# A fused long-convolution and gated-GLU kernel: fewer inverse-stage matmuls by combining complex products on VectorE, other places for the up copies, and a new instruction order

## The chip, the cores and the metric

The kernel runs on one core of a Trainium2 chip. The metric is the device time of one execution in microseconds (us). A core has five engines with a queue each: TensorE (PE in the profile, its weight loads PEld), VectorE (DVE), ScalarE (ACT), GpSimd (POOL) and SyncE (SP). Each works through its own queue in order and waits at semaphores for the others. A chip can give TensorE less than its full clock. Runs in which it did so markedly, or that took over 1.5% longer than the fastest run of their kernel, are "slow", and are not compared with "fast" ones.

## The reference, cut to what matters

```python
xn = layernorm(q)                                  # 2048 x 640
# A: causal long convolution over the 2048 tokens, per channel, by FFT
kv = shift_conv(k, shift_k) * v
y  = irfft(rfft(pad(kv)) * rfft(pad(ssm_k)))[:2048] + kv * ssm_D
# B: gated GLU, inner width 1728
h  = sigmoid(xn @ w_gate) * (xn @ w_up)
out = q + xn * y + h @ w_down
```

## The kernel before: what the change touches

**Part A** is a two-step DFT done with matmuls, for ten groups of 64 channels (an index `idx` from 0 to 9). Stage 1 (products of 32 rows) and stage 2 (of 64 rows) go forward. Then VectorE multiplies the spectra of `kv` and of the filter. The inverse stage (128 rows) and the last stage (32 x 32 tiles) go back. **Part B** is done for four blocks of 512 tokens, with 14 chunks of the inner width each: five matmuls for gate, five for up, a sigmoid on ScalarE, a multiply on VectorE, and after all chunks the down projection. The two parts are interleaved on TensorE by hand: part A's short runs stand between the projections of part B.

The product of two complex numbers needs `re*re - im*im` and `re*im + im*re`. The real parts lie in partitions 0 to 63 and the imaginary ones in 64 to 127. Without `ZC`, VectorE makes only the four real products, and the inverse stage adds them up in its accumulation, with two matmuls per output. With `ZC`, VectorE also does the subtraction and the addition, in halves of 64 partitions, and one matmul is enough:

```python
def rec_prod(idx, pri):
    ...                                        # Q = re*im and im*re into buffer P
    for b in range(2):
        dve(n, 2, lambda b=b: nc.vector.tensor_tensor(X(b), X(b), H(b), ALU.mult), ...)
    if idx in PRM["ZC"]:
        for b in range(2):
            dve(n, 2, lambda b=b: nc.vector.tensor_tensor(X(b)[0:64], X(b)[0:64], X(b)[64:P], ALU.subtract), ...)
            dve(n, 2, lambda b=b: nc.vector.tensor_tensor(X(b)[64:P], Q(b)[0:64], Q(b)[64:P], ALU.add), ...)

def rec_st3(idx, pri):                         # the inverse stage
    ...
            for j in range(JS):
                nc.tensor.matmul(o, lhsT=tl[S_][:, b, 0, j, :], rhs=Ab[:, 2 if zc else 0, :], start=True, stop=zc)
                if not zc:
                    nc.tensor.matmul(o, lhsT=tl[Z][:, b, j, :], rhs=Ab[:, 1, :], start=False, stop=True)
```

There is one buffer `P` for products. Without `ZC` it is held until the inverse stage has read it; with `ZC` only until VectorE has combined it.

An up projection is either multiplied straight from its PSUM bank, or first copied into the GLU buffer `hT` and multiplied there. The copy lets the bank go without waiting for VectorE:

```python
elif fc in PRM["UP"] and PRM["UP0"] <= pri < PRM["UP1"]:
    act(512, ...sigmoid -> sig...)
    ev(512, lambda: hT[:, fc, :], lambda: pv(1), ...)                              # the copy
    dve(512, 2, ...tensor_tensor(hT[:, fc, :], sig, hT[:, fc, :], ALU.mult)...)
else:
    act(512, ...sigmoid -> sig...)
    dve(512, 1, ...tensor_tensor(hT[:, fc, :], sig, pv(1), ALU.mult)...)           # straight from PSUM
```

Gate and up share two projection banks (`g`); part A has three double banks (`c`).

The order is not found by the kernel at run time. Two lists of numbers, `ORDER` and `ON_DVE`, say in which order about 950 operations are recorded, and which evictions VectorE takes in place of ScalarE. A buffer or bank is handed to the next user in the recorded order.

## Time and profile before

| | before |
|---|---|
| time, median of 3 runs | 268.5 us (267.57 to 269.28) |
| profiled run | span 268.0 us, clock 0.997, fast |
| TensorE, VectorE, ScalarE busy | 252.1, 181.6, 166.4 us |
| projections of blocks 0, 1, 2, 3 | 30.7, 46.6, 46.3, 46.3 us |
| down projections of blocks 0, 1, 2 | 15.8, 23.9, 21.4 us |

The trace has only 4336 of the 4375 matmuls (39 records of projections are missing), so its busy time of TensorE is somewhat low. A stage here goes from the start of a block's first projection matmul on TensorE's timeline to the start of its first down matmul, or from that to the next block.

The prediction below shows the lines of busy shares, slices and groups. Two more views are used later. First, TensorE's waits: what waited, for which engine, buffer and line; then us in total, the number of waits, and the longest.

```profile
PE g L766 <- DVE hT L733: 1.7, 2, 1.4
PE g L766 <- issue: 1.3, 8, 0.2
PE g L766 <- ACT sig L731: 1.0, 2, 0.7
```

The eight "issue" waits of 0.16 us are no waits: each stands before a run that is one record short of a multiple of five, so a missing record of the trace leaves the hole. Second, the busy time by engine in the projections of blocks 1 and 3: window, length, busy us of TensorE, its weight loads, VectorE, ScalarE and GpSimd with their counts, then clock, DMA share and GB/s.

```profile
61.64:108.26 46.62, 44.49 (x830) 25.48 (x839) 45.59 (x86) 38.74 (x51) 0.00 (x0) 1.00 0.65 162
199.83:246.17 46.34, 45.39 (x965) 27.39 (x975) 23.90 (x35) 30.62 (x41) 0.00 (x0) 1.00 0.30 76
```

In block 1 VectorE is busy for 45.6 of 46.6 us, as full as TensorE. In block 3 it has half its time free.

### The profile page before, as it was taken

How to read it: one execution, taken by the hardware profiler on the slowest of the kernel's cores; microseconds unless marked ns; L12 is line 12 of the kernel's file. 1: busy time of each engine (PE TensorE's matmuls, PEld its weight loads, DVE VectorE, ACT ScalarE, POOL GpSimd, SP SyncE). 2: the span in 40 equal slices, each digit the busy share in tenths (PEclk: the TensorE clock that was granted, in tenths of full speed). 3: DMA queues.
4: the chain of work that ended last, by engine and by line, in shares of the span. 5: the costliest groups of instructions: out<-in, count | busy, mean ns of one | idle time of the engine just before them, and what ended most of it. 6: DMA issues, size and time to landing. Idle time of an engine off the chain costs nothing.

```text
span 268.0 us, 9684 instructions
## 1 busy us (share of the span) xinstructions
PE 252.1 (94%) x4336; PEld 156.3 (58%) x4375; DVE 181.6 (68%) x319; ACT 166.4 (62%) x245; POOL 0.7 (0%) x6
## 2 busy tenths in 40 slices
PE   8899967998999999899999999999999999999993
PEld 3754434774445665677755555577676655555672
DVE  5333375269999999987799988695725853535831
ACT  3644945996499989674357649554477785644200
POOL 1000000000000000000000000000000000000000
PEclk9999999999999999999999999999999999999998
DMA  6999999999937516999954146677723075301741
GB/s 179 326 292 215 230 201 214 156 152 209 227 114 249 96 33 192 181 153 147 140 170 136 62 83 194 166 213 101 192 87 81 5 198 156 76 2 41 185 129 48
DMA packets 90449, 40.41 MB, mean 151 GB/s; under 512 B 66592, under 2 KB 88040, under 8 KB 90088
## 3 DMA queue, kind: packets, MB, share of 16 engines
q1 hardware_dynamic: 90216, 39.47, 69.0%
q8 instruction: 34, 0.56, 0.9%
q10 hardware_dynamic: 192, 0.33, 0.4%
q14 instruction: 7, 0.06, 0.1%
HBM read 30.61 MB, written 5.24 MB: 134 GB/s over the span
## 4 chain that ended last, share of the span: by engine, by line
PE 57%; SPq 14%; DVE 13%; DMA 10%; issue 3%; ACT 0%; DVEq 0%
PE g L766 23%; PE g L782 15%; PE c L523 6%; SPq L445 6%; DMA acc<-in_A_q_dram 4%; PE c L607 4%; DMA w<-in_B_w_gate_dram 3%; DVE ta L473 3%; PE c L503 2%; PE c L575 2%; SPq L412 2%; DVE P L553 2%; PE c L577 2%; PE g L812 2%; DMA ht<-in_A_ssm_k_dram 2%
## 5 line engine op out<-in xcount | busy, mean ns | idle before, releaser
L766 PE MATMUL g<-xnT,w 128*128 128x512 bf16 x348 | 86.3, 379 | 4.8 <-DVE hT L733 1.4
L782 PE MATMUL g<-wd,hT 128*128 128x320 bf16 x448 | 64.9, 299 | 0.0
L766 PEld LDWEIGHTS <-w 128*128 128x128 bf16 x380 | 34.5, 98 | 40.1 <-issue 3.7
L782 PEld LDWEIGHTS <-hT 128*128 128x128 bf16 x448 | 42.3, 98 | 16.5
L316 ACT CAST S<-c 128x1024 bf16<-128x1024 f32 x33 | 32.7, 1020 | 16.1 <-PE c L523 16.1
L733 DVE TENSOR_TENSOR hT<-sig,g 128x512 bf16<-128x512 bf16 x32 | 21.9, 685 | 17.7 <-PE g L766 11.9
L766 PE MATMUL g<-xnT,V 128*128 128x512 bf16 x133 | 31.2, 379 | 1.3 <-DVE acc L794 0.4
L794 DVE TENSOR_TENSOR acc<-g,acc 128x320 bf16<-128x320 f32 x32 | 15.6, 489 | 24.5 <-PE g L782 24.4
L731 ACT ACTIVATE sig<-g 128x512 bf16<-128x512 f32 x32 | 19.2, 600 | 18.8 <-PE g L766 14.9
L523 PEld LDWEIGHTS <-Mt 64*128 64x128 f16 x1280 | 20.2, 95 | 10.6 <-issue 10.2
L523 PE MATMUL c<-T,Mt 64*128 64x64 bf16 x1280 | 23.4, 190 | 0.8 <-DVE S L317 0.8
L316 ACT CAST V<-c 128x1024 bf16<-128x1024 f32 x19 | 18.6, 1014 | 7.9 <-PE c L577 7.8
L766 PEld LDWEIGHTS <-V 128*128 128x128 bf16 x140 | 13.3, 97 | 16.5 <-issue 1.5
L575 PE MATMUL c<-At,S 128*128 128x128 f16 x160 | 19.6, 219 | 0.5 <-DVE S L556 0.3
L316 ACT CAST T<-c 128x1024 bf16<-128x1024 f32 x18 | 17.6, 1023 | 3.2 <-PE c L503 3.2
L577 PE MATMUL c<-At,P 128*128 128x128 f16 x160 | 19.6, 219 | 0.0
L725 ACT ACTIVATE sig<-g 128x512 bf16<-128x512 f32 x18 | 10.8, 602 | 10.9 <-PE g L766 9.8
L575 PEld LDWEIGHTS <-S 128*128 128x128 bf16 x160 | 15.5, 98 | 2.5 <-DVE S L556 1.5
L319 ACT ACTIVATE T<-c 128x1024 bf16<-128x1024 f32 x14 | 13.9, 1024 | 3.9 <-PE c L503 3.9
L577 PEld LDWEIGHTS <-P 128*128 128x128 bf16 x160 | 15.7, 98 | 0.9
L728 DVE TENSOR_TENSOR hT<-sig,hT 128x512 bf16<-128x512 bf16 x18 | 7.5, 424 | 12.6 <-ACT hT L316 12.5
L553 DVE TENSOR_TENSOR P<-S 64x1024 bf16<-64x1024 bf16 x20 | 13.7, 686 | 1.2 <-PE c L577 0.7
(85 smaller groups left out, 264.8 us busy)
## 6 DMA issues: line engine op xcount, KB each, us to landing
w<-in_B_w_gate_dram SPq DMA_DIRECT2D x7, 640.0 KB, 6.6
w<-in_B_w_up_dram SPq DMA_DIRECT2D x7, 640.0 KB, 4.8
kt<-in_A_k_dram SPq DMA_DIRECT2D x8, 320.0 KB, 6.0
vt<-in_A_v_dram SPq DMA_DIRECT2D x8, 320.0 KB, 6.7
xnd<-xq SPq DMA_DIRECT2D x4, 640.0 KB, 3.9
P<-S SPq DMA_DIRECT2D x10, 256.0 KB, 3.7
ht<-in_A_ssm_k_dram SPq DMA_DIRECT2D x16, 96.0 KB, 5.2
wd<-in_B_w_down_dram SPq DMA_DIRECT2D x3, 480.0 KB, 9.6
```

The lines of the kernel that those rows point to most:

```text
L316: fa = lambda: nc.scalar.copy(out=out_fn(), in_=in_fn())
L319: fa = lambda: nc.scalar.activation(out_fn(), in_fn(), ACT.Copy, scale=scale)
L445: dma(lambda e, g=g, p=p, c0=c0: e.dma_start(tl[b][g * N1:(g + 1) * N1, :, p, :], h3[:, c0 + j0:c0 + j1, :]), 32 * (j1 - j0), 128, w=[(b, ...
L523: nc.tensor.matmul(tl[c][:, b, 64 * kk:64 * kk + 64], lhsT=Mb[rows, k, 64 - 64 * r:192 - 64 * r], rhs=tl[T][rows, 2 * k + r].rearrange("p ...
L553: dve(n, 2, lambda a=a, o=o, b=b: nc.vector.tensor_tensor(Q(b)[a], X(b)[a], H(b)[o], ALU.mult), r=sr + ([(Z, b, 1)] if h else []), w=[(Z, ...
L575: nc.tensor.matmul(o, lhsT=tl[S_][:, b, 0, j, :], rhs=Ab[:, 2 if zc else 0, :], start=True, stop=zc)
L577: nc.tensor.matmul(o, lhsT=tl[Z][:, b, j, :], rhs=Ab[:, 1, :], start=False, stop=True)
L731: act(512, lambda: nc.scalar.activation(tl[sg][:], pv(0), ACT.Sigmoid), r=[pk(0)], w=[(sg,)], alloc=[(sg, "sig")], pri=pri - 2000)
L733: dve(512, 1, lambda: nc.vector.tensor_tensor(hT[:, fc, :], tl[sg][:], pv(1), ALU.mult), r=[pk(1), (sg,)], w=[(hk, fc)], pri=pri - 2000)
L766: nc.tensor.matmul(tl[c][:], lhsT=w()[:, k, o:o + P], rhs=tl[X][:, k, :], start=(k == 0), stop=(k == NC - 1))
L782: nc.tensor.matmul(tl[pd[i]][:, 0:320], lhsT=hT[:, fc, t4 * P:(t4 + 1) * P], rhs=wd[:, fc, 320 * i:320 * i + 320], start=(fc == 0), stop=( ...
L794: dve(320, 1, lambda i=i, m=m, pd=pd: nc.vector.tensor_tensor(acc[:, m, 320 * i:320 * i + 320], tl[pd[i]][:, 0:320], acc[:, m, 320 * i:320 ...
```

## The change

It has two intents. The first is to take 96 matmuls off TensorE and give 24 operations to VectorE, where that has room. The second is to put the up copies where they help. Both go with a wholly new recorded order.

```diff
-               SWAP=(5, 6, 7, 8, 9), UP=(1, 3, 5, 7, 9, 11), UP0=60.0, UP1=230.0, ZC=())
+               SWAP=(5, 6, 7, 8, 9), UP=(0, 1, 2, 3, 4, 5, 6, 7, 8, 9, 10, 11, 12), UP0=130.0, UP1=230.0,
+               ZC=(4, 5, 6, 7, 8, 9))
...
-            pe(490, 32, f, ...
+            pe(460, 32, f, ...          # estimates of durations: they set priorities; ORDER fixes the order
...
-    MG, MD = 215.2, 136.5    # the priorities that follow from these are what UP0 and UP1 are compared with
+    MG, MD = 213.5, 135.0
...
 ORDER = [
-    6, 0, 5, 1, 4, 2, 8, 7, 42, 11, 10, 13, 12, 9, 3, 14, 16, 71, 72, 15, 73, 74, 75, 91, 17, 86, 76, 96, 77, 104,
...
+    3, 6, 0, 5, 42, 1, 4, 2, 8, 7, 11, 10, 13, 12, 9, 14, 16, 71, 72, 15, 73, 74, 75, 91, 17, 86, 76, 96, 77, 104,
...                                      # the whole list differs; ON_DVE goes from 30 to 26 entries
```

Before, the odd chunks of blocks 1, 2 and 3 were copied (18 copies). After, chunks 7 to 12 of block 2 and all 13 full chunks of block 3 are (19 copies), and none in block 1.

## The prediction

> **What bounds the kernel now.** I read the page's busy shares and slices first, then the costliest groups, then the timeline of TensorE, then the waits.
>
> ```profile
> PE 252.1 (94%) x4336; PEld 156.3 (58%) x4375; DVE 181.6 (68%) x319; ACT 166.4 (62%) x245; POOL 0.7 (0%) x6
> ...
> PE   8899967998999999899999999999999999999993
> ...
> DVE  5333375269999999987799988695725853535831
> ACT  3644945996499989674357649554477785644200
> ...
> L733 DVE TENSOR_TENSOR hT<-sig,g 128x512 bf16<-128x512 bf16 x32 | 21.9, 685 | 17.7 <-PE g L766 11.9
> ...
> L316 ACT CAST V<-c 128x1024 bf16<-128x1024 f32 x19 | 18.6, 1014 | 7.9 <-PE c L577 7.8
> ...
> L577 PE MATMUL c<-At,P 128*128 128x128 f16 x160 | 19.6, 219 | 0.0
> ...
> L728 DVE TENSOR_TENSOR hT<-sig,hT 128x512 bf16<-128x512 bf16 x18 | 7.5, 424 | 12.6 <-ACT hT L316 12.5
> L553 DVE TENSOR_TENSOR P<-S 64x1024 bf16<-64x1024 bf16 x20 | 13.7, 686 | 1.2 <-PE c L577 0.7
> ```
>
> TensorE is busy in nearly every slice. Slices 10 to 17 (60 to 115 us) have VectorE full as well: there the two bind together. After slice 24 (160 us) VectorE is at 30 to 80% and TensorE alone sets the pace. So a TensorE instruction removed late is worth its whole issue time, and VectorE work added there is nearly free.
>
> "Busy" hides how fast matmuls issue, so I took start-to-start times from the timeline of TensorE.
>
> ```profile
> 115.63 0.22 PE L577 MATMUL c<-At,P 128*128 128x128 f16 x1
> 115.69 0.22 PE L575 MATMUL c<-At,S 128*128 128x128 f16 x1
> ...
> 149.75 3.40 PE L766 MATMUL g<-xnT,w 128*128 128x512 bf16 x15
> 153.08 0.64 PE L523 MATMUL c<-T,Mt 64*128 64x64 bf16 x32
> 153.65 0.69 PE L607 MATMUL c<-V,Bt 32*32 32x80 bf16 x64
> ...
> 201.00 1.57 PE L523 MATMUL c<-T,Mt 64*128 64x64 bf16 x96
> 202.51 1.25 PE L766 MATMUL g<-xnT,w 128*128 128x512 bf16 x4
> 203.60 1.11 PE L782 MATMUL g<-wd,hT 128*128 128x320 bf16 x7
> ```
>
> The 128-column matmuls of the inverse stage start 0.056 us apart (32 of them fill 115.57 to 117.36). The 219 ns of the group table is latency, not cost. The stage-2 runs show a fixed cost: 32 take 0.57 us, 96 take 1.51, so 0.0147 each and 0.10 per run. A projection run of 15 ahead of such a run takes 3.33 us where 15 at 213 ns are 3.20 (213 ns is the pace of the first block: 60 matmuls between 15.15 and 27.89 us). The projection run ahead of a down projection (five matmuls, one record missing) takes 1.09 and has no such surplus. I read it as about 0.11 us for going over to a run of 32- or 64-row products, and about as much once per stage-2 run.
>
> Real waits of TensorE are few. The largest pair is at the end of block 0:
>
> ```profile
> 37.14 1.02 PE L766 MATMUL g<-xnT,w 128*128 128x512 bf16 x4 [0.69 <-ACT sig L731]
> 39.59 3.40 PE L766 MATMUL g<-xnT,w 128*128 128x512 bf16 x15 [1.42 <-DVE hT L733]
> ```
>
> VectorE's timeline says why: the multiply of chunk 10 stands behind the 13 small instructions of the reciprocal root (35.96 to 38.5 us), which stand behind a table copy that waited for its load until 34.98. Other waits sum to about 6 us, the end after the last matmul to about 4.
>
> **What the Trainium skill says.** "TensorE: Matmul & The Clock Gate", section "Back-to-back issue gap", gives N/2.4 + 2.5 ns warm: 55.8 for 128 columns, where the trace has 56; for 512 it gives 216, the trace 213, and I use the trace. "Perfetto Trace Analysis", "Identifying the Most-Contended Engine", says matmul busy share is a poor measure because pipelined instructions overlap; the trace agrees (219 against 56). "VectorE: DVE Perf Modes", "Walkthrough: the 8-slice pipeline in each mode", has a two-tensor operation at two 16-bit elements per cycle at best, and at one with a PSUM operand. The trace agrees: 512 columns cost 424 ns from SBUF (L728) and 685 from PSUM (L733), and 64 partitions (L553) cost the same 686 ns as 128 (L556), so the half-height operations that the change adds are not cheap. "ScalarE: Activation LUTs", "What ACT_TABLE_LOAD costs", gives 186 + 0.833 N ns: 612 for 512 columns; the trace's up copies take 594.
>
> **The change part by part.** It is the diff's parameters, plus a wholly new instruction order. I counted instructions of both built programs per engine and multiplied by the durations above.
>
> 1. Complex product combined on VectorE for groups 4 to 9. Each inverse-stage unit goes from 16 to 8 matmuls, two units per group, six groups: 96 matmuls and 96 weight loads fewer; x 0.056 = **-5.4 us of TensorE**. VectorE gets 24 operations of 64x1024: x 0.686 = +16.5 us. Each group's chain from stage 2 to the inverse stage grows by 4 x 0.69 = 2.75 us, which hurts only if TensorE gets there first. The order puts the inverse stage of groups 5 to 9 well after the last stage-2 run of its group (12 to 38 us of TensorE work between), group 4 about 11.5 us.
>
> 2. Up copies. Before, six odd chunks of each of blocks 1, 2, 3 (18). After, none of block 1, six of the later chunks of block 2, all 13 of block 3 (19). One more copy on ScalarE, 0.6 us; one multiply of 0.424 for one of 0.685 on VectorE. The total hardly moves; the place does.
>
> 3. Evictions. VectorE gives up 4 stage-2, 5 stage-1 and some small ones and takes others, and takes three normalisations from ScalarE. With parts 1 and 2, VectorE's sum is 181.6 -> about 190.7, ScalarE's 166.4 -> about 171. Neither is near 260. In block 1's projections VectorE loses four evictions of 1.22, six multiplies of 0.424 and some others: about 8 us less where it was full. That stretch (61.6 to 108.3 us) holds about 45 us of TensorE work in 46.6: worth **-1.0 us**.
>
> 4. Order. Runs of TensorE work go from 158 to 134. Entries into 32- or 64-row runs fall from 53 to 39, stage-2 runs from 26 to 20: 20 x 0.11 = **-2.2 us**. The reciprocal root of block 0 no longer has the table copy ahead of it and its statistics end before chunk 10's sigmoid, so the wait of 2.1 us should shrink to 0.8: **-1.3**. Against it: two memsets (0.33 + 0.27) now precede the one that the warm-up matmuls need, and TensorE's start sets the first transposes: **+0.6**.
>
> 5. New waits. Input rows (about 1 MB) now load ahead of weights for chunks 4 to 7. With about 4 MB moved by 15 us in the trace before, these weights should land near 17 us, needed at 19.5; tight. Longer VectorE chains will also miss some slots. I allow **+1.3**.
>
> Sum: -5.4 - 1.0 - 2.2 - 1.3 + 0.6 + 1.3 = -8.0, so 268.5 -> 260.5 us.
>
> **Rivals.** First: VectorE becomes the bound. For it: it is at 95 to 99% from 60 to 110 and around 140 us, and gets 9 us more. Against: the additions fall from 115 us on, mostly where it idles, and block 1 is relieved. If group 4 and 5 run late, 264 to 267. Second: ScalarE. It takes 7 big evictions net and statistics in one lump during the first down projection; late sigmoids hold the two projection banks. Against: 62% busy, and its sum grows by under 5 us. If so, 263 to 265. Third: loads in the first 30 us come late, since the queues are full there; up to 3 us, about 263. Fourth: the order works better than I allow and no new wait appears: 258.
>
> **Range and chances.** The 5.4 us are an instruction count and alone are 2.0%, just at the limit; the run count adds 2.2 with a less sure unit. For less than 2% (above 263.1 us) new waits must eat about 3.9 us where I allow 1.3. I give 257.5 to 264.0; faster 0.77, same 0.20, slower 0.03.
>
> **What would show it.** Matmuls of the inverse stage 224 instead of 320, still 56 ns apart; TensorE busy near 245 us with its last slices unchanged; projections of block 1 about 2 us shorter; the wait near 37 us under 1 us; the first transpose at 6.9 instead of 6.28 us; no wait of TensorE on the combining operations above 1 us in total. It is wrong if TensorE waits several us on them or on projection banks, if single matmuls start further than 56 ns apart (weight loads of 98 ns binding), or if weights come late near 19 us.

## The result, and the profile after

The changed kernel took 259.97 us in the median of four runs, against 268.89 us for the kernel before in the same rounds. The result is correct. One of the four runs, the profiled one, was slow: 357.06 us at a mean granted clock of 0.661. The three fast ones took 257.36, 258.83 and 261.11 us. The ratio of the fast runs is 0.964, with an interval of 0.954 to 0.974: faster. All ratios here are those of the record, from fast runs of the same rounds, so not quite the ratio of the medians that are quoted. The prediction was 260.5 us, 257.5 to 264.0; the median of the three fast runs is 258.83.

As the first profile was slow, the changed kernel was run again, and all profile lines of "after" are from that run.

> The changed kernel again, because its first profile fell in the slow state. Theory (TensorE sets the pace, 96 matmuls and about 20 run entries fewer): 257.4 to 261.1 us as in the fast runs so far, ratio about 0.964; TensorE busy about 245 us; inverse-stage matmuls still 0.056 us apart; first transpose 0.6 us later than before (6.9); the wait near 37 us under 1 us; block 1's projections 2 us shorter than 46.6. Rival (the gain is removed waits, not removed matmuls): TensorE busy stays near 250 and its idle time falls by over 5 us.

Measured: 258.61 us (257.82 to 260.29), ratio 0.959 (0.951 to 0.967), profile fast with a span of 258.5 us. Line numbers of the changed kernel are two higher in its body (L766 is now L768, L577 is L579, and so on).

The page: busy shares, the slices, and groups.

```profile
PE 245.9 (95%) x4279; PEld 151.6 (59%) x4279; DVE 191.9 (74%) x339; ACT 169.9 (66%) x250; POOL 0.7 (0%) x6
...
PE   7889997999999999999999998999999999999993
...
DVE  5424364557899999988998789779978696959631
...
L735 DVE TENSOR_TENSOR hT<-sig,g 128x512 bf16<-128x512 bf16 x31 | 21.2, 686 | 17.3 <-PE g L768 17.3
...
L577 PE MATMUL c<-At,S 128*128 128x128 f16 x160 | 15.0, 219 | 0.4 <-issue 0.3
...
L579 PE MATMUL c<-At,P 128*128 128x128 f16 x64 | 7.8, 219 | 0.0
```

The inverse stage is 160 matmuls of the first kind, with 64 of the second kind left: 224 for 320. They still start about 0.055 us apart (eight of them fill 203.60 to 204.04). VectorE is now at 70% or more in 18 of the 24 slices after the sixteenth, where it had been in 13, and after the start TensorE's row of nines is broken only by one seven and one eight. The waits of TensorE:

```profile
PE g L814 <- DVE sig L803: 1.8, 1, 1.8
PE c L525 <- issue: 1.7, 1, 1.7
PE c L748 <- ACT sig L733: 0.8, 1, 0.8
PE g L768 <- ACT sig L733: 0.4, 1, 0.4
```

No wait on the combining operations (L562 and L564) is among them. The wait on the multiply hT is down from 1.7 to 0.2 us. New are a wait for the first sigmoid (L748) and one named "issue" in the middle of a stage-2 run. All listed waits together are 8.0 us; before they were 8.3 without the holes of missing records. So the 9.5 us between the two spans are hardly less waiting, they are less work on TensorE, and the rival named above for a1_after does not hold. The windows of blocks 1 and 3:

```profile
60.46:104.73 44.27, 44.04 (x842) 25.40 (x839) 41.67 (x79) 38.31 (x47) 0.00 (x0) 1.00 0.81 177
197.97:237.25 39.28, 39.26 (x762) 21.81 (x759) 30.88 (x49) 26.34 (x39) 0.00 (x0) 1.00 0.37 98
```

In both, TensorE's busy time is within 0.3 us of the length. Block 1's projections became 2.35 us shorter. Block 3's fell by 7.1 us, of which 3.1 reappear in the down projection of block 2, which took over some of its part-A work. The start is later, on the other hand: block 0's projections begin at 16.30 instead of 15.15 us. From the timeline of TensorE (start, length, work, and in brackets the idle time before it and its releaser):

```profile
6.89 0.74 PE L702 MATMUL c<-ident,xq 128*128 128x128 bf16 x5
...
15.47 1.00 PE L748 MATMUL c<-xnT,V 128*128 128x128 bf16 x15 [0.77 <-ACT sig L733]
...
153.64 0.93 PE L525 MATMUL c<-T,Mt 64*128 64x64 bf16 x51
156.26 0.83 PE L525 MATMUL c<-T,Mt 64*128 64x64 bf16 x45 [1.69 <-issue]
```

The first transpose starts at 6.89, as predicted. The second line was not predicted: the last matmuls of the first chunks are recorded behind the first sigmoid, which stands on ScalarE behind a table load (1.28 us in this trace). The last two lines are one run of 96 matmuls, cut in two by a wait that no semaphore explains; more on it below.

### The profile page after: what moved, and what is told of

Its sections match the earlier page's. It is cut to its first block, busy times and chain, and to the rows that moved or that the text cites. A ratio compares the mean times of both kernels' runs of the same rounds, so it can differ in the third digit from the quotient of the medians.

```text
span 355.3 us, 9555 instructions
## 1 busy us (share of the span) xinstructions
PE 346.1 (97%) x4279; PEld 185.5 (52%) x4279; DVE 193.9 (55%) x339; ACT 171.9 (48%) x250; POOL 0.7 (0%) x6
## 4 chain that ended last, share of the span: by engine, by line
PE 97%; ACT 1%; DVE 0%; issue 0%
PE g L768 48%; PE g L784 26%; PE c L525 8%; PE c L577 4%; PE c L505 3%; PE c L609 3%; PE g L814 2%; PE c L748 2%; PE c L579 1%; ACT xnT L317 1%; PE c L702 0%; ACT sig L733 0%; PE g L702 0%; ACT sig L722 0%; DVE acc L796 0%
## 5 line engine op out<-in xcount | busy, mean ns | idle before, releaser
L768 PE MATMUL g<-xnT,w 128*128 128x512 bf16 x380 | 128.8, 510 | 0.3 <-ACT sig L733 0.3
L784 PE MATMUL g<-wd,hT 128*128 128x320 bf16 x448 | 94.4, 387 | 0.0
L768 PEld LDWEIGHTS <-w 128*128 128x128 bf16 x380 | 43.9, 120 | 66.4 <-issue 64.5
L784 PEld LDWEIGHTS <-hT 128*128 128x128 bf16 x448 | 51.5, 118 | 35.0 <-issue 0.4
L735 DVE TENSOR_TENSOR hT<-sig,g 128x512 bf16<-128x512 bf16 x31 | 21.3, 687 | 47.6 <-PE g L768 47.3
L768 PE MATMUL g<-xnT,V 128*128 128x512 bf16 x140 | 46.7, 510 | 0.0
L525 PEld LDWEIGHTS <-Mt 64*128 64x128 f16 x1280 | 25.6, 104 | 10.0 <-issue 9.3
L768 PEld LDWEIGHTS <-V 128*128 128x128 bf16 x140 | 16.1, 119 | 25.7 <-issue 24.5
L525 PE MATMUL c<-T,Mt 64*128 64x64 bf16 x1280 | 28.4, 210 | 0.0
L320 ACT ACTIVATE T<-c 128x1024 bf16<-128x1024 f32 x18 | 17.8, 1025 | 6.8 <-PE c L505 6.8
L317 ACT CAST hT<-g 128x512 bf16<-128x512 f32 x19 | 11.1, 586 | 19.8 <-PE g L768 19.8
L577 PE MATMUL c<-At,S 128*128 128x128 f16 x160 | 20.7, 265 | 0.0
L577 PEld LDWEIGHTS <-S 128*128 128x128 bf16 x160 | 15.9, 118 | 3.8 <-issue 2.8
L470 DVE TENSOR_TENSOR tb<-kt,sT 128x1024 bf16<-128x1024 bf16 x20 | 13.7, 687 | 1.6 <-ACT kt L317 1.4
```

The costliest lines, as they stand in the source:

```text
L317: fa = lambda: nc.scalar.copy(out=out_fn(), in_=in_fn())
L320: fa = lambda: nc.scalar.activation(out_fn(), in_fn(), ACT.Copy, scale=scale)
L470: dve(1024, 2, lambda: nc.vector.tensor_tensor(tl[c][:], sl(tl[kb], 3 - m), sh(m), ALU.mult) if c != o else nc.vector.tensor_tensor(tl[c]. ...
L525: nc.tensor.matmul(tl[c][:, b, 64 * kk:64 * kk + 64], lhsT=Mb[rows, k, 64 - 64 * r:192 - 64 * r], rhs=tl[T][rows, 2 * k + r].rearrange("p ...
L735: dve(512, 1, lambda: nc.vector.tensor_tensor(hT[:, fc, :], tl[sg][:], pv(1), ALU.mult), r=[pk(1), (sg,)], w=[(hk, fc)], pri=pri - 2000)
L768: nc.tensor.matmul(tl[c][:], lhsT=w()[:, k, o:o + P], rhs=tl[X][:, k, :], start=(k == 0), stop=(k == NC - 1))
```

## The experiments

Theory: TensorE sets the pace from end to end, so the gain is the 96 matmuls, plus fewer visits to runs of 32- or 64-row products, plus a few waits; copies and order only have to keep new waits away. The rival is that one part alone, the order or the placing of the copies, makes the gain, or that the combining has a price on the path. A third view came up on the way: that the parts cannot be valued one by one.

All results, with the lengths of the projections of blocks 1, 2 and 3 from each profile:

| run | what it is | median us | ratio to before | 1 | 2 | 3 |
|---|---|---|---|---|---|---|
| before | | 268.5 | | 46.6 | 46.3 | 46.3 |
| a1_after | the changed kernel | 258.61 | 0.959 | 44.3 | 46.3 | 39.3 |
| a2_pe16 | after, 96 matmuls given back | 266.13 | 0.987 | 44.3 | 47.4 | 42.0 |
| b1_zc | before + combining, old order | 284.62 | 1.057 | 46.6 | 48.8 | 53.0 |
| b2_zclate | the same, inverse stages later | 299.64 | 1.117 | 46.6 | 53.5 | 63.4 |
| b3_up | before + new copies, old order | 273.46 | 1.016 | 50.0 | 48.9 | 46.4 |
| a3_order | new order, neither | 290.91 | 1.072 | 48.9 | 62.2 | 52.8 |
| a9_nozc | new order + new copies, no combining | 273.47 | 1.017 | 44.3 | 56.0 | 43.0 |
| a4_upold | new order + combining, old copies | 274.12 | 1.023 | 49.2 | 49.2 | 45.6 |
| a5b_noup | after without any copy | 273.58 | 1.017 | 44.3 | 49.5 | 49.0 |
| a7_up1 | after + copies of block 1 | 266.10 | 0.986 | 49.7 | 45.7 | 39.3 |
| a8_split | after, 8 more visits to 32-row runs | 262.32 | 0.976 | 44.3 | 46.3 | 39.5 |
| a6_start | after, earlier start | 258.49 | 0.964 | 44.3 | 48.5 | 39.3 |

Two of the four runs of a3_order, the profiled one among them, were slow, so its stages are only a hint; its ratio is from the fast runs (288.16 and 289.16 us). All other profiles in the table are fast; that of a1_after is of the slowest of its four runs (260.29 us). Where a part was brought into an order that was made without it, some operations had to be recorded earlier, since otherwise a buffer or bank never comes free. Such kernels are not the part alone; they are the part in a repaired order.

### The 96 matmuls given back (a2_pe16)

```diff
+                    if zc:
+                        nc.tensor.matmul(o, lhsT=tl[S_][:, b, 0, j, :], rhs=Ab[:, 2, :], start=True, stop=True)
                     nc.tensor.matmul(o, lhsT=tl[S_][:, b, 0, j, :], rhs=Ab[:, 2 if zc else 0, :], start=True, stop=zc)
```

Each matmul of the six groups is done twice, with the same result; combining, order and copies stay.

> The changed kernel with the 96 matmuls given back as doubles (each product of groups 4 to 9 issued twice into the same place, the second overwrites, so the result is right); VectorE's combining stays. Theory (TensorE bound): 96 x 0.056 = 5.4 us slower than the changed kernel, so about 264. Rival (these stages wait for VectorE anyway, or the gain is in the order): under 2.5 us slower.

Measured: 266.13 us, 7.5 more than the changed kernel in the same rounds; by the two profiles 265.1 - 258.5 = 6.6. Stage by stage from the traces: 16 more inverse matmuls in block 2's projections lengthened them by 1.1 us, 32 in its down projection by 2.3, 48 in block 3's projections by 2.67 (48 x 0.056 = 2.69). Block 3 has no listed wait in either trace, so that stage prices the matmul alone. The sum of the 0.056s is 5.4. The rest of the 6.6 (1.2) is mostly waits: a new one for an up copy in block 2 and one near the end,

```profile
168.33 3.40 PE L770 MATMUL g<-xnT,w 128*128 128x512 bf16 x15 [0.96 <-ACT hT L317]
...
251.82 8.45 PE L786 MATMUL g<-wd,hT 128*128 128x320 bf16 x61 [1.12 <-issue]
```

and a longer "issue" wait in the down projection of block 2 (0.79 instead of 0.32 us); against them stand shorter "issue" waits in block 2 (1.6 instead of 2.1) and a start 0.5 us earlier. So the theory's term holds at its unit, and the matmuls carry 5.4 of the 9.8 us between the two medians (268.44 and 258.61 in those rounds) directly.

### Combining in the old order (b1_zc, b2_zclate)

```diff
-  ... UP=(1, 3, 5, 7, 9, 11), UP0=60.0, UP1=230.0, ZC=())
+  ... UP=(1, 3, 5, 7, 9, 11), UP0=60.0, UP1=230.0, ZC=(4, 5, 6, 7, 8, 9))
 # ORDER: the four combining operations of a group right behind its products
```

> The kernel before with only the combining on VectorE for groups 4 to 9, each group's four operations put right behind its products in the old order. Theory: 5.4 us of TensorE less, but the old order has the inverse stage close behind the products of group 4 and VectorE full until 150 us, so 1 to 3 us come back as waits: 264 to 267. Rival one (VectorE not in the way at all): 263. Rival two (VectorE's 16.5 us bind): 268 or more.

Measured: 284.62 us, 16 us slower than before, though it has the same 96 matmuls fewer. My expectation failed badly; even the rival's "268 or more" was mild. The waits of TensorE, first line:

```profile
PE c L577 <- DVE S L564: 10.7, 6, 2.9
```

The inverse stages stand where products alone would have been ready. Each group's chain is 4 x 0.69 us longer, and TensorE stops for it, up to 2.9 us at a time. All listed waits of TensorE are 23.3 us, against 9.6 before. The clock adds to it: the trace has it at 0.50 in two stretches of 3.4 us, worth at most 3.4 of the 16 us. The wait on the combining is what the prediction had feared for groups 4 and 5, and the new order does not have it. So I made the inverse stages of groups 4 to 9 later by three items of TensorE's queue:

> As b1_zc (the old order, combining on VectorE for groups 4 to 9), but the inverse stages of these groups stand three TensorE work items later. Theory (what cost b1_zc 14 us is the longer chain from product to inverse stage, met by an inverse stage that stood right behind it): waits of TensorE on the combining fall from 24 us to under 8 and the time to 268 to 274. Rival (VectorE's added 16.5 us bind by their amount): still 280 or more.

Measured: 299.64 us. (The 24 us in the expectation are nearly all listed waits of TensorE in b1_zc; those on the combining were the 10.7 above.) The aimed-at waits fell to about 1 us, and the kernel became slower still. The waits of ScalarE tell why (same columns as above, with ScalarE waiting):

```profile
ACT V L318 <- PE c L577: 37.3, 10, 9.0
```

ScalarE's evictions of the inverse stage kept their old places in its queue, to within one. They now waited 37.3 us for the later matmuls, the sigmoids behind them waited too, and TensorE stopped for projection banks. I conclude that an operation cannot be moved on one engine alone: each queue is in order, and the whole neighbourhood has to move. A run with the neighbourhood moved as well was not made. The theory fell, and with it any hope of pricing the combining by itself in the old order. The clock of this profile was 0.96: it was at 0.50 in five stretches, 24 us in all, so up to 12 of the 31 us are clock.

### New copies in the old order (b3_up), and the order without the combining (a3_order, a9_nozc)

```diff
 # b3_up: the kernel before
-  ... UP=(1, 3, 5, 7, 9, 11), UP0=60.0, UP1=230.0, ZC=())
+  ... UP=(0, 1, ..., 12), UP0=131.0, UP1=230.0, ZC=())
 # ORDER: 8 multiplies or sigmoids recorded earlier, so that the two projection banks come free
```

> The kernel before, its own order, with only the up copies of the changed kernel (block 2 from chunk 7, all of block 3; none in block 1); 16 matmuls per inverse unit, no combining. Eight evictions or multiplies are recorded a few places earlier, because the two projection banks would otherwise not come free. The copies were worth much inside the new order (without those of blocks 2 and 3: 273.6 us; with those of block 1 added: 266.1). If they carry a gain of their own: 263 to 267 us. Rival, from the two earlier tries to bring one part alone into an order made for another (284.6 and 290.9): the old order has its copies where its own ScalarE and VectorE queues leave room, block 1 and the first half of block 2 lose them, and the time rises to 272 us or more, with waits of TensorE on multiplies in blocks 1 and 2. I hold the rival the likelier.

Measured: 273.46 us; the rival was right. Its window of block 1, to be read against the first window line of before:

```profile
60.50:110.46 49.96, 45.64 (x842) 25.76 (x839) 48.22 (x88) 36.23 (x45) 0.00 (x0) 1.00 0.59 147
```

Without its copies block 1 gives VectorE 48.2 us of work where it had 45.6, and the stage is 3.3 us longer. In the old order VectorE was at its limit there, and the copies were what relieved it. Block 3 has 13 copies instead of 6 and takes 46.35 us as before (46.34): TensorE alone sets that stage, so a copy has nothing to give.

```diff
 # a3_order: the changed kernel's ORDER with the work of before
-  UP=(0, 1, ..., 12), UP0=130.0, UP1=230.0, ZC=(4, 5, 6, 7, 8, 9))
+  UP=(1, 3, 5, 7, 9, 11), UP0=60.0, UP1=230.0, ZC=())
 # a9_nozc: only ZC=() ; in both, about a dozen operations recorded earlier because P is held longer
```

> The work of the kernel before (no combining, the up copies of before) in the order of the changed one; the single P buffer forces the inverse stages of groups 5 and 8 and a few evictions some places earlier. Theory: run entries, block 1's relief and the shorter root wait stay, the 5.4 us are lost: 264 to 267. Rival (the new order is most of the gain): 262 or less.

> The changed kernel with part 1 undone: 96 matmuls given back as real products, the 24 combining operations gone, copies and order kept. Without the combining the one product buffer is held until the inverse stage has read it, so nine operations are recorded earlier than in the changed kernel, among them a last-stage unit and the inverse stages of groups 5 and 8. If the order only works because the combining frees the product buffer early, TensorE waits for evictions and banks in blocks 2 and 3 and the whole is 272 us or more, against 266.1 for the kernel that gave the same matmuls back and kept the combining. Rival: the combining is worth just its matmuls, 265 to 268 us.

Measured: 290.91 us and 273.47 us. a3_order missed what I expected of it (264 to 267) by a wide margin, which is why I expected 272 or more for a9_nozc; in its slow trace TensorE waits 10.0 us for multiplies that read PSUM (L735). a9_nozc came in beside a2_pe16 as the comparison: both have 320 inverse matmuls, in nearly the same order and with the same copies; a2_pe16 combines and takes 266.1 us, a9_nozc does not and takes 273.5. In this order the 24 operations of VectorE are thus worth some 7 us beyond the matmuls they save.

My number was met, but not my reason: I had expected waits for evictions and banks. In a9_nozc P is held until the inverse stage, so an inverse stage and a last-stage unit had to be recorded early and crowd block 2's projections: 56.0 us, where the changed kernel has 46.3. They hold 48 more inverse matmuls (2.7 us) and 128 more last-stage ones (about 1.2), and the listed waits are 5.7 us instead of 2.1. Of these, 4.8 are waits named "issue", and only 0.9 are for evictions. Around them the clock was halved (a window line as above):

```profile
168.50:175.30 6.80, 4.84 (x36) 3.52 (x34) 0.00 (x0) 0.64 (x1) 0.00 (x0) 0.50 0.22 59
```

That is worth at most 3.4 us; all four runs had a clock of 0.986 to 0.991. So the combining frees the one product buffer early, and that lets the new order put the inverse stages late: this the repair itself shows. How the 7 us divide into crowding, "issue" waits and clock is not shown. A second product buffer would be the cleaner test, and was not run.

### The copies in the new order (a4_upold, a5_noup, a5b_noup, a7_up1)

> The changed kernel with the up copies of before (odd chunks of blocks 1, 2, 3, 18 in all) in the new order, each copy right ahead of its multiply. Theory: block 1, where ScalarE and VectorE are both nearly full, gets six copies back and waits on them, 2 to 5 us there; 260 to 264. Rival (where the copies stand does not matter, their sum hardly changes): within 1 us of the changed kernel, 258 to 260.

The edit puts the UP and UP0 of before into the changed kernel, each copy recorded just ahead of its multiply. Measured: 274.12 us. The direction was as the theory had it, the size several times as large. Block 1 (copies added) took 4.9 us more and block 3 (even chunks without copy) 6.3 more. The next runs take the two apart.

a5_noup was to have no copy at all:

> The changed kernel without any up copy: every multiply reads the up half from PSUM. ScalarE gets 11 us less, VectorE 5 us more (19 x (0.685 - 0.424)). Theory: in blocks 2 and 3 TensorE sets the pace and both engines have room, so 257 to 261, the copies are worth under 2 us. Rival (the copies free the projection banks earlier, and TensorE would wait for them): 262 or more, with waits of TensorE on the multiply.

It did not build. The file that I handed in was the one in which the projection banks never come free, not the mended one, so it is a build and no run. The mended one:

```diff
-  UP=(0, 1, ..., 12), UP0=130.0, UP1=230.0,
+  UP=(), ...
 # ORDER: 5 multiplies recorded one or two places earlier
```

> The changed kernel without any up copy: the 19 copies of blocks 2 and 3 go, and VectorE multiplies straight from the projection bank there too (685 ns for 424 ns each, +5.0 us of VectorE, -11.3 us of ScalarE). If the copies of block 3 let the projection banks go earlier and so carry part of the gain, the projections of block 3 take about 45 us or more where the changed kernel has 39.3, and the whole is 264 to 268 us. Rival: the copies only move work between two engines that have room, and it stays within 1.5 us of the changed kernel, 257.5 to 260.

Measured: 273.58 us, 15.0 more than the changed kernel by the medians, 12.1 by the profiles, and more than the first expectation allowed. Block 2's projections took 3.2 us more, block 3's 9.7. Three lines of TensorE's timeline in block 3:

```profile
213.81 1.24 PE L768 MATMUL g<-xnT,w 128*128 128x512 bf16 x5 [2.68 <-DVE hT L735]
...
227.29 1.24 PE L768 MATMUL g<-xnT,w 128*128 128x512 bf16 x5 [0.69 <-ACT sig L733]
...
240.23 2.32 PE L768 MATMUL g<-xnT,w 128*128 128x512 bf16 x10 [0.85 <-DVE hT L735]
```

Nine such waits add up to 7.9 us, and TensorE's busy time in the stage rises by 1.5 us for the same matmuls, about 0.2 per restart. In the first line VectorE had four operations of 0.69 us in its queue, one of them a combining one, ahead of the multiply that would have freed the bank. Here copies and combining are coupled: VectorE may take the 24 operations late because the copies, on ScalarE, let the banks go without it.

Now the copies of block 1 alone:

```diff
-        elif fc in PRM["UP"] and PRM["UP0"] <= pri < PRM["UP1"]:
+        elif fc in PRM["UP"] and PRM["UP0"] <= pri < PRM["UP1"] or tr == 1 and fc % 2 and not last:
```

> The changed kernel with nothing but the six odd up copies of block 1 put back (+3.6 us of ScalarE, -1.6 us of VectorE, in block 1 alone). The run that gave all copies of before to the new order (274.1 us) lengthened the projections of block 1 by 4.9 us and those of block 3 by 6.3. If the block 1 part of that was the copies of block 1, the projections of block 1 take 48 to 49 us instead of 44.3, the other stages keep their lengths, and the whole is 262 to 264 us. Rival: the lengthening of block 1 came from elsewhere, and it stays within 1 us of the changed kernel.

Measured: 266.10 us, 7.5 more than the changed kernel by the medians, 5.7 by the profiles. Block 1's projections took 49.7 us (48 to 49 expected), the other projections kept their lengths to within 0.7 us. The whole was expected at 262 to 264, so it came out higher. The lines that show how a copy hurts, from the timeline of all engines:

```profile
87.94 0.58 ACT L318 CAST hT<-g 128x512 bf16<-128x512 f32 x1
...
88.55 0.43 DVE L731 TENSOR_TENSOR hT<-sig,hT 128x512 bf16<-128x512 bf16 x1 [3.89 <-ACT hT L318]
88.57 1.24 PE L769 MATMUL g<-xnT,w 128*128 128x512 bf16 x5 [0.42 <-ACT hT L318]
...
91.65 1.02 PE L769 MATMUL g<-xnT,w 128*128 128x512 bf16 x4 [1.50 <-DVE hT L736]
```

The copy stands on ScalarE behind stage-1 and stage-2 evictions of 1.0 us each. VectorE waits 3.9 us for it, all its later work is late by that, and TensorE stops 1.5 us for a multiply two chunks on. An "issue" wait of 1.15 us that ends at 86.70 stands at the start of this chain, so not all of it is the copy's. a4_upold, which has these copies too, has such a wait at the same place of the program (0.69 us), and no other kernel here; whether the copies bring it about is open. The same six copies that were needed in the old order (b3_up lost 3.3 us without them) are harmful in the new one.

### The price of going over to small products (a8_split)

```diff
 # ORDER: in each of the 8 pairs of last-stage runs, the second run (64 matmuls) goes behind the next projection or down run
```

> The changed kernel with the second half of each of the eight pairs of last-stage runs (64 matmuls of 32 rows each) moved behind the next projection or down run, so that 8 more runs of 32- or 64-row products are entered; no work is added. At the 0.11 us per entry that the prediction used it is +0.9 us on TensorE, spread over stages of blocks 2 and 3; if going back costs as much again, +1.7. Expected: 259.3 to 260.5 us, matmuls busy about the same count. Rival: entries cost nothing and the saving by fewer runs was not there: within 0.5 us of the changed kernel.

Measured: 262.32 us; by the profiles 260.9 - 258.5 = 2.4 us more. Listed waits account for 0.6 of them (1.05 us for a residual add near the end, less elsewhere), which leaves 1.8 for eight visits. One of the pairs, first in the changed kernel:

```profile
174.58 1.22 PE L609 MATMUL c<-V,Bt 32*32 32x80 bf16 x128
175.73 3.02 PE L784 MATMUL g<-wd,hT 128*128 128x320 bf16 x21
```

and split:

```profile
174.53 0.69 PE L610 MATMUL c<-V,Bt 32*32 32x80 bf16 x64
175.15 1.12 PE L785 MATMUL g<-wd,hT 128*128 128x320 bf16 x7
176.21 0.69 PE L610 MATMUL c<-V,Bt 32*32 32x80 bf16 x64
```

128 matmuls together take 1.15 us from start to the next start, two halves 0.62 each: 0.09 more. And the seven down matmuls in front of the second half take 1.06 us (175.15 to 176.21), where seven at the trace's 0.135 would be 0.95: 0.11 more. So a visit costs about 0.2 us, half on the way in and half in the run. The higher of the two entry costs (+1.7) was right by the profile. By the medians the difference is 3.7 us, and the expected 259.3 to 260.5 us were missed; the 1.3 beyond the profiles' is not explained by any line I have read.

### An earlier start (a6_start)

The memset that the warm-up matmuls need is recorded first, and the first sigmoid after the last matmuls of its bank.

> The changed kernel with its first instructions mended: the memset that the warm-up matmuls need goes first again, and the first sigmoid is recorded after the last matmuls of its own tile, so that these do not wait for it. Theory: TensorE starts 0.6 us earlier and the 0.77 us wait at 15.5 us goes; the projections of block 0 start at about 15.0 instead of 16.3 us, and all of it reaches the end: 257.3, against 258.6. Rival (block 0 waits for loads or statistics later on, which absorb it): 258.5.

Measured: 258.49 us, no measurable gain. The projections of block 0 start at 14.68 us instead of 16.30, and block 2's still start 1.3 us earlier (125.88 instead of 127.20). Then the "issue" wait of block 2 takes 2.24 us instead of 1.69, and behind it the clock is at 0.50 for 3.4 us (156.8 to 160.2). So the rival's 258.5 was met, but not by what it named. In the runs of this kernel with a clock of 0.999 or more the times are 257.44, 257.72 and 258.50. So the repair does what it should at the start, and it is lost to something later that I did not control.

### The waits named "issue"

They came back in every kernel but b1_zc, at up to 2.24 us, and no engine or DMA of the kernel releases them. One line of the page of a1_after lists a queue of instructions:

```profile
q8 instruction: 33, 0.54, 0.9%
```

These are 33 transfers of 16,384 bytes (the queue's number, its packets, MB, and their share of the DMA engines). TensorE's trace has 8,558 instructions, matmuls and weight loads together, and 8,558 / 33 is 259 for each, close to 256. I then looked for the place in TensorE's program at which each wait of 0.25 us or more falls, counted by weight loads, of which no trace here lacks any (two instructions for each). Of 32 such waits in 13 traces, 31 fall at a place between 170 and 184 in counting modulo 256, and 15 of them at exactly 176. The other one is of 0.33 us, in b2_zclate. By chance some 2 of 32 would fall into such a stretch of 15. The kernels share most of their order, so these are not 31 independent cases, but they are eight different borders. So these waits come at one place in each block of 256 instructions of the program. The 1.69 us wait of a1_after began at 154.57; a 16 KB transfer had started at 154.0 and took 0.96 us, the one before it 11.6 us earlier. Near most of them, ahead, stand runs in which a matmul and its weight load take 9 to 15 ns together (128 last-stage matmuls in 1.15 us, 96 stage-2 ones in 1.51), so that 256 instructions would go by in 1.2 to 1.9 us. That TensorE outruns its supply of instructions there fits all of this, but it is inferred, not shown: moving the place, by other lengths of runs ahead of it, was not tried, as it came too late in the study.

## Why the prediction was right, point by point

- **The 96 matmuls, -5.4.** Right. a2_pe16 shows 0.056 us each, in the stages where they stand, and 1.2 us more of waits, net, that came with them. In a1_after they still start about 0.055 us apart, so their weight loads of 0.098 us do not bind. The formula that the prediction took from the skill for this is not its figure for such a stream; see the last section.
- **The combining costs TensorE nothing.** Right for this order: no wait on L562 or L564. b1_zc shows that this is a property of the order, not of the operations: 10.7 us of waits elsewhere. VectorE's sum came to 191.9 (about 190.7 predicted), ScalarE's to 169.9 (about 171). The prediction misread one row, though: after slice 24 VectorE had been between 10% and over 90%, not at 30 to 80%.
- **Copies, "The total hardly moves; the place does".** The count was right, the value of the place was missed. I gave it no term. In the new order, 12 to 15 us hang on the copies of blocks 2 and 3 (a5b_noup, by profiles and by medians) and 6 to 7.5 on there being none in block 1 (a7_up1). I saw the copy as 0.6 us on an engine with room, and not as what frees a projection bank.
- **Relief of block 1, -1.0.** The stage fell by 2.35. VectorE's work there fell by 3.9 us (45.6 to 41.7), not by about 8: the six multiplies counted as gone came back from PSUM at 0.686 each, and three evictions went, not four. The reason I gave, less work on the full VectorE, isn't enough: with its copies put back in a7_up1, VectorE had still less to do (40.3 us), and the stage was 5.4 us longer. Of the 2.35, about 0.7 are waits (listed ones fell from 1.45 to 0.23 us, but 0.5 of the former were missing records) and about 0.6 are three visits fewer at 0.2. The rest stays open.
- **Order, 20 x 0.11 = -2.2.** Mis-sized. The unit belongs to both ends of a visit: about 0.2 us (a8_split), and visits fell from 53 to 39, so 14 x 0.2 = 2.8.
- **The wait on the reciprocal root, -1.3.** 2.11 us before, 0.41 after at the same place: -1.7.
- **The memsets, +0.6.** The first transpose is at 6.89 instead of 6.28, as predicted. The projections start 1.15 us later; the sigmoid behind the table load adds to it, which I hadn't seen.
- **New waits, +1.3.** Leaving out the root and the missing records, TensorE's listed waits went from about 6.2 to 7.6 us: +1.4 for the 1.9 I had allowed with the memsets. That the allowance nearly fits is luck, for they are not the ones I named. No weight came late near 19 us, and no VectorE chain was missed. It was the first sigmoid and the "issue" wait.

With these, -5.4 - 2.8 - 1.7 + 1.4 = -8.5; the two profiled spans differ by 9.5. About 1.0 us I can't assign; it is as much as stays open in block 1. The 2.8 is an estimate, from a unit measured on last-stage runs alone.

None of the rivals came about in the changed kernel. But each partial kernel shows one of them: VectorE as the bound (b1_zc, and b3_up in block 1), ScalarE's queue holding sigmoids (b2_zclate), banks held by multiplies (a5b_noup). What the prediction treated as separate terms of a sum isn't one. Combining alone 284.6, copies alone 273.5, order alone 290.9 (288.2 and 289.2 in its fast runs), and the two pairs that were run 273.5 and 274.1: all slower than the 268.5 of before, and only the three together are faster. Since moved operations had to be mended into foreign orders, these figures also contain the misfit. The sum came out because I counted the two final programs, not the parts; that the new order would bring no waits on copies and banks was allowed for in one lump, not worked out.

## What to carry to other kernels

Where one engine sets the pace from end to end, count its instructions in both final programs at their start-to-start spacing, add the switches between shapes at what the trace shows for them, and price everything else only by the waits it makes. Do not value a scheduling choice, such as a copy that frees a bank, in another order than its own: the same six copies gained 3.3 us in one and lost up to 5.4 in the other. And when moving an operation, follow it into the queue of every engine that touches its result, or the engine you did not move will hold the others up.

## What the Trainium skill lacked or had wrong

- "TensorEngine Tiling (Array Packing)", section "Key Properties", says that changing the tiling mode drains TensorE, but gives no cost. Here a visit to a run of 32-row products costs about 0.2 us (0.11 in the run before it, 0.09 in the run itself; a8_split), and by that unit 14 visits fewer are an estimated 2.8 us.
- "Runtime: NRT & Kernel Launch", section "Instruction fetch mechanics", has instructions refilled in blocks of 16 KiB, 256 instructions each, and calls the cost of crossing such a border mostly hidden. The size agrees with this case (33 transfers of 16,384 bytes for 8,558 instructions). If the waits named "issue" are this cost, which is inferred and not shown, it is not hidden here: up to 2.24 us (a6_start), 31 of 32 waits within one stretch of 15 places modulo 256.
- "TensorE: Matmul & The Clock Gate", section "Back-to-back issue gap", gives the formula that the prediction used for a matmul on its own only, and for a stream of weight loads and matmuls about 81 ns (128 columns) and 131 ns (512). In this case, where every matmul has its own weight load, they start 56 and 213 ns apart (before).
